# Attention and two MLP layers in one kernel on one core: another planner for the order of the instructions

## The chip, the core and the metric

The kernel runs on one core of one Trainium2 chip. A core has a matrix engine (TensorE, PE in the rows; its weight loads have a row name of their own, PEld), a vector engine (VectorE, DVE), an activation engine (ScalarE, ACT), a general engine (GpSimd, POOL), a queue that issues the transfers (SyncE, SP) and 16 DMA engines. SBUF is the on-chip memory that all of them reach; PSUM is the small memory that TensorE writes its products to, in eight banks.

The metric is the device time of one execution in microseconds (us). Three runs of the kernel before gave 600.65, 600.74 and 601.78 us; the median is 600.74 us.

## What is computed

The input is a small linear attention with a decay per head (2 batches, 8 heads, 768 positions, 64 values per head), whose output, 1536 tokens of 512 values, goes through two MLP layers with 2048 hidden values each:

```
for b in range(nb):                                  # blocks of 64 positions
    intra = einsum('bhic,bhjc->bhij', qb, kb) * Dmask
    intra = einsum('bhij,bhjd->bhid', intra, vb)
    inter = einsum('bhid,bhde->bhie', qb * lam_pow, kv_state)
    out[:, :, sl] = intra + inter
    kv_state = lam_block * kv_state + einsum('bhsd,bhse->bhde', kb * rev_pow, vb)
...
h = x @ moe_w_in                                     # layer 1
x = (h * tanh(softplus(h))) @ moe_w_out
h = maximum(x @ moe2_w_in, 0.0)                      # layer 2
x = (h * h) @ moe2_w_out
```

The weights are made by `np.random.randn(...) * ...` and reach the kernel as 64-bit floats; the kernel turns each into a 32-bit float itself.

## The kernel before

**Products in two halves.** Every operand x of a large product is kept as a rounded part (h) and the rest (l = x - h), and `mm3` (L186 to L191) makes one product out of three matrix products, h·h, h·l and l·h. Making the two parts is called a split: ACT casts x to h, and DVE or POOL subtracts (`split`, L241 to L245).

**Weights.** A slice of weights is 128x512 numbers of 64 bits (512 KB). `bits` (L220) loads it into one of five `raw` buffers and makes 32-bit floats in place, in four steps that follow each other: CA on ACT (L230, a scaled copy of the high word to `absw`), CB on DVE (L232, the low word shifted right by 29), CC on DVE (L234, the two put together), CD on DVE (L236, the sign). There are 64 slices, so each of these lines runs 64 times. A slice is then split (L243, L244).

**Attention.** `pair(i)` (L316) does two heads of one block of 384 positions: loads `kq` and `kv` (L379, L381), scores S (L340), scaling of k by powers of lambda on ACT (L344), of q on POOL (L348), updates U of the state (L334), masks on DVE (L351), the state's steps on DVE (L362, L364), outputs V (L373, L375), and the split of the result into `xh` (L400, ACT) and `xl` (L402, DVE). There are 16 pairs. The powers of lambda (`dT`, `qs`) are made on DVE by scans (L308, L309) out of `lam_t`, a 4 KB load (L297) that gives every partition the same eight numbers. Four pairs make one block of tokens `x`, which the first product of layer 1 needs.

**MLP.** Half of layer 1 (eight slices, 32 steps of `h_step`, `g_step`, `y_step`, L431 to L464) is done plainly, the first 16 steps in between the attention. The other half of layer 1 and all of layer 2 go in 24 quads (class `Quad`, L556): a 2x2 block of products of weights and tokens made with seven products p1 to p7 in place of eight, at the price of sums ahead of them (`paired` L258 for weights; `first_factors` L499 and `next_factors` L526 for tokens) and behind them (`add`, L588, DVE, which reads the product's PSUM bank). Behind the sums come the activation on ACT (L596) and the split of its result (`low`, L599; h on ACT at L606 or L609, l at L610 on DVE or POOL). The order of the seven products stands in `self.order` (L561), one for quads that are `turned` (every second of layer 1) and one for the others, layer 2 among them. Between a quad's products stand the output products (`y`) of the quad before, which are summed up by L425 on DVE. Products of layer 2 take turns in two PSUM banks, so a product waits until the sum of the one before it in that bank has read it.

**What sets the order.** No instruction is issued as the code is read. `op` (L113) records each with its engines and a duration for each, and the places that it reads and writes. `issue` (L132) then goes through all with a clock of its own: it gives each operation a due time, counted back from those that wait for it, and emits, engine by engine, the one with the earliest due time among those ready within SLACK (0.25 us). Where two engines are allowed it takes the one on which the operation starts first. Every engine then runs its instructions strictly in that order, each waiting for the semaphores of what it depends on. In this planner each engine is on its own: nothing says that an operation of DVE and one of POOL can hold each other up.

## Time and profile before

| | |
|---|---|
| median of three runs | 600.74 us |
| profiled execution | 601.85 us, span 599.9 us |
| TensorE busy | 577.1 us (96% of the span), 3448 matmul records |
| VectorE busy | 428.6 us (71%), 705 instructions |
| ScalarE busy | 319.5 us (53%), 662 instructions |
| GpSimd busy | 254.0 us (42%), 241 instructions |
| DMA | 49.88 MB, 24.4% of the 16 engines' span |

The profile is of one execution. Busy time of an engine is the union of its instructions' spans. A matmul's record begins when it starts and its end is modelled, so two that follow each other overlap in the record, and the idle time that the profile gives between two of them is somewhat less than what TensorE lost. The granted clock of TensorE (PEclk) is a share of 2.4 GHz: 1.00 is 2.4 GHz, 0.5 would be 1.2 GHz, and a number between them means that a stretch had some of both.

The kernel has four stages: attention with 16 steps of layer 1 woven in (0 to about 125 us), the other plain steps and the eight quads of layer 1 (to about 330 us), the passage to layer 2, in which layer 1's sums are finished and split again as layer 2's tokens (about 315 to 375 us), and the 16 quads of layer 2 (to the end).

### The profile page before, as it was taken

What the parts mean: (1) busy time and instruction counts of PE and PEld (TensorE: products, weight loads), DVE (VectorE), ACT (ScalarE), POOL (GpSimd) and SP (SyncE); (2) the same over time, 40 slices, a digit from 0 to 9 for tenths busy, and PEclk for the clock granted to TensorE, in tenths of its full rate; (3) what the DMA queues carried; (4) which work ended last, traced back from release to release, by engine and by line L of the source; (5) the groups of instructions that cost most, each with busy time, mean ns of one, the idle gap of its engine ahead of it and who ended that gap; (6) DMA issues with size and microseconds to landing.
All of it is one profiled execution on the core that took longest, in us unless ns stands there. A gap on an engine that the chain in (4) does not pass through costs nothing.

```text
span 599.9 us, 9221 instructions
## 1 busy us (share of the span) xinstructions
PE 577.1 (96%) x3448; PEld 528.8 (88%) x3448; DVE 428.6 (71%) x705; ACT 319.5 (53%) x662; POOL 254.0 (42%) x241
## 2 busy tenths in 40 slices
PE   6789999999999999999999988999999899999997
PEld 5668888889999999999999877889988789899886
DVE  3988477789873888569879999789458935633433
ACT  2554445466433545355465667867575655544441
POOL 2467244566680354125478595554115423100010
PEclk8899999999999999999999989999999999999999
DMA  8866553222000412023200311242120120100112
GB/s 291 311 184 212 169 161 115 72 71 72 0 1 1 176 36 71 2 73 138 72 0 1 116 60 35 72 175 61 47 105 2 70 107 1 35 1 0 54 52 107
DMA packets 15741, 49.88 MB, mean 83 GB/s; under 512 B 1872, under 2 KB 1872, under 8 KB 15696
## 3 DMA queue, kind: packets, MB, share of 16 engines
q1 hardware_dynamic: 15696, 49.29, 24.4%
q8 instruction: 27, 0.44, 0.3%
q14 instruction: 18, 0.15, 0.1%
HBM read 46.14 MB, written 3.15 MB: 82 GB/s over the span
## 4 chain that ended last, share of the span: by engine, by line
PE 72%; DVE 14%; POOL 5%; issue 4%; DMA 3%; ACT 1%; SPq 0%; POOLq 0%; DVEq 0%; ACTq 0%
PE y L189 10%; PE y L190 10%; PE y L191 9%; PE h L189 9%; PE h L191 9%; PE h L190 8%; PE X L190 2%; PE Y L189 2%; PE Y L191 2%; PE X L191 2%; PE Y L190 2%; PE X L189 2%; POOL w L244 2%; DVE u L590 2%; DVE raw L236 2%
## 5 line engine op out<-in xcount | busy, mean ns | idle before, releaser
L244 POOL TENSOR_TENSOR w<-raw,w 128x256 fp32r<-128x256 f32 (+1 forms) x72 | 82.7, 1155 | 79.8 <-ACT w L243 69.3
L590 DVE TENSOR_TENSOR u<-h,u 128x384 f32<-128x384 f32 x88 | 48.8, 554 | 55.8 <-PE h L191 55.2
L189 PE MATMUL h<-xh,w 128*128 128x384 f32 x244 | 83.7, 343 | 1.6 <-ACT w L243 1.1
L190 PE MATMUL h<-xl,w 128*128 128x384 f32 x244 | 82.9, 340 | 1.9 <-DVE xl L402 1.8
L191 PE MATMUL h<-xh,w 128*128 128x384 f32 x244 | 82.8, 339 | 1.0 <-POOL w L244 1.0
L596 ACT ACTIVATE u<-u 128x384 f32<-128x384 f32 x72 | 37.9, 527 | 72.0 <-DVE u L590 71.3
L189 PE MATMUL y<-gh,w 128*128 128x384 f32 x192 | 66.8, 348 | 0.2
L190 PE MATMUL y<-gl,w 128*128 128x384 f32 x192 | 64.6, 336 | 0.8 <-POOL gl L449 0.8
L243 ACT CAST w<-raw 128x256 fp32r<-128x256 f32 (+1 forms) x96 | 48.7, 523 | 29.3 <-DVE raw L236 20.4
L191 PE MATMUL y<-gh,w 128*128 128x384 f32 x192 | 64.3, 335 | 0.0
L234 DVE SCALAR_TENSOR_TENSOR raw<-absw,raw 128x512 uint32<-128x512 uint32 x64 | 56.9, 889 | 6.5 <-ACT absw L230 2.4
L610 POOL TENSOR_TENSOR g<-u,g 128x384 fp32r<-128x384 f32 x20 | 21.2, 1058 | 94.5 <-PE h L191 80.4
L236 DVE SCALAR_TENSOR_TENSOR raw<-raw 128x512 uint32<-128x512 uint32 x64 | 55.8, 872 | 1.0
L230 ACT ACTIVATE absw<-raw 128x512 f32<-128x512 f32 x64 | 43.0, 676 | 17.3 <-DVE raw L234 7.1
L189 PEld LDWEIGHTS h<-xh,w 128*128 128x128 f32 x244 | 46.1, 189 | 6.5 <-issue 1.2
L190 PEld LDWEIGHTS h<-xl,w 128*128 128x128 f32 x244 | 46.1, 189 | 5.0 <-DVE xl L402 2.6
L191 PEld LDWEIGHTS h<-xh,w 128*128 128x128 f32 x244 | 46.2, 189 | 1.6 <-POOL w L244 1.6
L425 DVE TENSOR_TENSOR y<-y,y 128x384 f32<-128x384 f32 (+1 forms) x72 | 39.6, 571 | 9.5 <-PE y L191 9.0
L232 DVE TENSOR_SCALAR raw<-raw 128x512 uint32<-128x512 uint32 x64 | 41.3, 646 | 2.4 <-DMA raw<-in_w2o_dram 2.2
L189 PEld LDWEIGHTS y<-gh,w 128*128 128x128 f32 x192 | 36.0, 187 | 3.1 <-DVE st L364 0.4
L190 PEld LDWEIGHTS y<-gl,w 128*128 128x128 f32 x192 | 36.1, 188 | 1.7 <-POOL gl L449 1.5
L449 POOL TENSOR_TENSOR gl<-u,gh 128x384 fp32r<-128x384 f32 x19 | 21.0, 1104 | 36.3 <-ACT gh L447 35.5
(266 smaller groups left out, 1514.3 us busy)
## 6 DMA issues: line engine op xcount, KB each, us to landing
raw<-in_w1i_dram SPq DMA_DIRECT2D x16, 512.0 KB, 4.2
raw<-in_w1o_dram SPq DMA_DIRECT2D x16, 512.0 KB, 3.9
raw<-in_w2i_dram SPq DMA_DIRECT2D x16, 512.0 KB, 4.4
raw<-in_w2o_dram SPq DMA_DIRECT2D x16, 512.0 KB, 3.8
kq<-in_qkv_dram SPq DMA_DIRECT2D x16, 384.0 KB, 4.8
kv<-in_qkv_dram SPq DMA_DIRECT2D x16, 384.0 KB, 3.3
out_dram<-y SPq DMA_DIRECT2D x12, 256.0 KB, 2.0
lam_t<-in_lam_dram SPq DMA_DIRECT2D x1, 4.0 KB, 6.8
```

The source lines that it names most:

```text
L189: pe.matmul(o, lhsT=wh, rhs=h, start=start, stop=False, **kw)
L190: pe.matmul(o, lhsT=wh, rhs=l, start=False, stop=False, **kw)
L191: pe.matmul(o, lhsT=wl, rhs=h, start=False, stop=stop, **kw)
L230: op("ACT", 0.68, lambda e: e.activation(absw[a].bitcast(F32), word.bitcast(F32)[:, :, 1], AF.Copy, scale=2.0 ** -112), R, A, after=after, ...
L232: op("DVE", 0.55, lambda e: e.tensor_scalar(lo, lo, 29, None, op0=ALU.logical_shift_right), [], R, after=last.get("bits", ()), name=f"CB{F ...
L234: op("DVE", 0.85, lambda e: e.scalar_tensor_tensor(lo, absw[a], 3, lo, ALU.logical_shift_left, ALU.bitwise_or), A, R, name=f"CC{F}.{io}")
L236: o = op("DVE", 0.85, lambda e: e.scalar_tensor_tensor(lo, hi, 0x80000000, lo, ALU.bitwise_and, ALU.bitwise_or), [], R, name=f"CD{F}.{io}")
L243: op("ACT", dur, lambda e: e.copy(v(h), v(t)), r, H_, name="H" + kw["name"])
L244: op(eng, 0, lambda e: e.tensor_tensor(v(l), v(t), v(h.bitcast(F32)), ALU.subtract), [*r, *H_], L_, due=kw.get("due", 1e9), name="L" + kw[ ...
L425: op("DVE", dur, lambda en: en.tensor_tensor(o, o, y, ALU.add), B, O, due=due, name=f"YD{layer}.{t}.{e}")
L590: op("DVE", 0.58, lambda e: e.tensor_tensor(o, a, b, ALU.add), [s for s in A + B if s not in O], O, name=f"add{self.n}")
L596: op("ACT", 0.52, lambda e: e.activation(o, i, fn), [s for s in I if s not in O], O, name=f"{name}.{self.n}")
```

## The change

Numbers of lines of the new kernel differ; the names are the same. Where rows of the new kernel are shown: L262 is the load of a weight slice (L227 before), L265 CA, L272 CB on ACT, L274 CB on DVE, L277 CC, L279 CD, L287 the subtraction of a split (L244), L315 the sums of `paired` (L272), L340 the load of lambda (L297), L351 and L352 the scans, L394 the masks, L405 and L407 the state's steps, L422 and L424 the loads of `kq` and `kv`, L443 and L445 the split into `xh` and `xl`, L468 the sums of outputs (L425), L575 those of `next_factors` (L532), L634 `add` (L590), L655 the l part behind an activation (L610).

1. The planner. Durations of single operations are set anew, most of them lower (TOP, SUB256, SUB384, SUB512, CC and CD). An operation that reads no PSUM bank is `shared`; a shared one on DVE or POOL may not begin before the shared one before it, on either of the two, has ended (less HEAD). TensorE is given 0.3 us after what it waits for (LATE), its results come 0.16 us later (TAIL), and the next instruction on an engine may begin somewhat before the end of the last (NEXT). An operation with two engines is kept off one of them where the other would end it sooner. All this is run for 27 sets of EARLY, SLACK and FAVOUR, and the order with the earliest end by the planner's clock is emitted.
2. CB may run on ACT too, as a scaled copy of the upper half of the low word (`top`), at 0.62 us there and 0.42 us on DVE.
3. The load of lambda comes ahead of the first `kq`.
4. The order of a quad's products in layer 1, with p7 and p5 next to each other; their sums now go by `both` and `sum`. Layer 2's order stays.
5. A split's buffer in a quad is taken from a list of free ones (`gfree`) and not in turn.

```diff
-LAT, LAND, SLACK = 0.2, 2.0, 0.25
+LAT, LATE, LAND, TAIL = 0.1, 0.3, 2.0, 0.16
+HEAD = {"DVE": 0.14, "POOL": 0.06}
+NEXT = {"PE": 0.0, "ACT": 0.1, "DVE": 0.08, "POOL": 0.04, "SP": 0.0, "-": 0.0}
...
-EARLY = 0.5
+EARLY, SLACK, FAVOUR = (0.0, 0.5, 1.0), (0.1, 0.25, 0.4), (0.0, 0.5, 1.0)
...
+        o.shared = not any(z[0] in bank for z in r) if shared is None else shared
...
+        def when(o, e, r):
+
+            r = max(r, free[e])
+            if o.shared and e in HEAD:
+                r = max(r, port - HEAD[e])
+            return r
...
+                for k in c[:]:
+                    for x, d in k[1].eng.items():
+                        if x != e and when(k[1], x, k[0]) + d + favour.get((x, e), 0) <= k[0] + k[1].eng[e]:
+                            c.remove(k)
+                            break
...
+            on[o], end[o] = e, r + o.eng[e] + (TAIL if e == "PE" else 0)
+            free[e] = r + o.eng[e] - NEXT[e]
+            if o.shared and e in HEAD:
+                port = free[e]
...
+        for early in EARLY:
+            for slack in SLACK:
+                for favour in FAVOUR:
+                    t, out = order(early, slack, {("DVE", "POOL"): favour, ("ACT", "DVE"): -0.3, ("DVE", "ACT"): 0.3})
...
+                    if best is None or t < best[0]:
+                        best = t, out
...
-    SUB384 = {"POOL": 1.1, "DVE": 0.6}
...
+    TOP = {"ACT": 0.62, "DVE": 0.42}
+    SUB384 = {"POOL": 1.01, "DVE": 0.55}
...
-        op("DVE", 0.55, lambda e: e.tensor_scalar(lo, lo, 29, None, op0=ALU.logical_shift_right),
-           [], R, after=last.get("bits", ()), name=f"CB{F}.{io}")
...
+        half = word.bitcast(U16)[:, :, 1]
+
+        def top(e):
+            if e is act:
+                e.activation(lo, half, AF.Copy, scale=2.0 ** -13, bias=2.0 ** -14 - 0.5)
+            else:
+                e.tensor_scalar(lo, lo, 29, None, op0=ALU.logical_shift_right)
+
+        op(TOP, 0, top, [], R, after=last.get("bits", ()), name=f"CB{F}.{io}")
...
-        o = op("SP", 1.05, lambda e: e.dma_start(out=kq[n4], in_=qkv_in[t, p, :, 0:2]), [], KQ, after=last.get("kq", ()), name=f"kq{i}")
+        o = op("SP", 1.05, lambda e: e.dma_start(out=kq[n4], in_=qkv_in[t, p, :, 0:2]), [], KQ, after=last.get("kq", last["lam"]), name=f"kq{i}")
...
-            self.order = ("p1", "p6", "p7", "p5", "p3", "p2", "p4") if turned else ("p1", "p6", "p2", "p7", "p4", "p5", "p3")
+            self.order = "p1 p6 p2 p7 p4 p5 p3" if layer else "p1 p6 p5 p7 p2 p3 p4" if turned else "p1 p6 p7 p5 p2 p4 p3"
...
-            (h, l), (H_, L_) = gsets[next_of("g", 4)]
+            k = gfree.pop(0)
+            (h, l), (H_, L_) = gsets[k]
...
+        def both(self):
+            if self.C and self.D:
+                r = self.t["r"]
+                self.add(r, self.D, r)
+                self.leave("c22", r, r)
```

**SP at the start.** The rows are the loads that SP issues first; before:

```order
L379 DMA kq_110<-in_qkv_dram 128x768
L381 DMA kv_114<-in_qkv_dram 128x768
L379 DMA kq_111<-in_qkv_dram 128x768
L297 DMA lam_t<-in_lam_dram 128x8
L381 DMA kv_115<-in_qkv_dram 128x768
```

and now:

```order
L340 DMA lam_t<-in_lam_dram 128x8
L422 DMA kq_110<-in_qkv_dram 128x768
L424 DMA kv_114<-in_qkv_dram 128x768
L422 DMA kq_111<-in_qkv_dram 128x768
L424 DMA kv_115<-in_qkv_dram 128x768
```

Lambda's load moved ahead of three loads; the others keep their order.

**DVE in the attention's first pairs**, from the first weight slice on (`raw_91`; `pm`, `mid` and `st` are masks and states of the pairs, `xl` the split result); before:

```order
L232 TENSOR_SCALAR raw_91<-raw_91 128x512
L351 TENSOR_TENSOR pm_123<-Y,dT 128x384
L364 SCALAR_TENSOR_TENSOR st_127<-mid_125,qs,y_136 64x64 x2
L362 COPY mid_125<-X 64x64
L308 SCALAR_TENSOR_TENSOR dT<-lam_t,g_108 128x128 x2
L309 SCALAR_TENSOR_TENSOR qs<-lam_t,g_108 128x128
L234 SCALAR_TENSOR_TENSOR raw_91<-absw_96,raw_91 128x512
L351 TENSOR_TENSOR pm_123<-X,dT 128x384
L364 SCALAR_TENSOR_TENSOR mid_125<-mid_125,qs,X 64x64 x2
L236 SCALAR_TENSOR_TENSOR raw_91<-raw_91 128x512
L402 TENSOR_TENSOR xl_83<-y_138,xh_79 128x384
L232 TENSOR_SCALAR raw_92<-raw_92 128x512
```

and now:

```order
L445 TENSOR_TENSOR xl_83<-y_136,xh_79 128x384
L394 TENSOR_TENSOR pm_123<-Y,dT 128x384
L407 SCALAR_TENSOR_TENSOR st_127<-mid_125,qs,y_136 64x64 x2
L394 TENSOR_TENSOR pm_123<-X,dT 128x384
L405 COPY mid_125<-X 64x64
L407 SCALAR_TENSOR_TENSOR mid_125<-mid_125,qs,X 64x64 x2
L277 SCALAR_TENSOR_TENSOR raw_91<-absw_96,raw_91 128x512
L279 SCALAR_TENSOR_TENSOR raw_91<-raw_91 128x512
L445 TENSOR_TENSOR xl_83<-y_138,xh_79 128x384
```

The shifts of the slices (L232) are gone from DVE here, and the last scans stand before these rows; ACT now has the shift of `raw0_91` between a scaling and a cast of the pairs:

```order
L387 ACTIVATE kv2_116<-kv2_116,dT_118 128x3x64 x2
L272 ACTIVATE raw0_91<-raw0_91 128x512
L443 CAST xh0_79<-y3_138 128x384
L405 COPY mid0_125<-X_133 64x64
L265 ACTIVATE absw1_97<-raw1_92 128x512
```

Of the 64 shifts ACT has 55 now (L272) and DVE 9 (L274); of the 24 that stood ahead of the first quad's first sum on DVE, three are left there. Of the 96 subtractions behind an activation in the quads, DVE had 44 and has 56, POOL had 52 and has 40. POOL's instructions go from 240 rows to 231, DVE's from 668 to 624. TensorE's instructions are the same in number and kind.

**DVE in the passage to layer 2**, between sums (`u`) that TensorE waits for; before:

```order
L590 TENSOR_TENSOR u2_100<-h0_131,u2_100 128x384
L532 TENSOR_TENSOR y1_88<-y1_88 128x384
L532 TENSOR_TENSOR y1_88<-y1_88,y0_87 128x384
L244 TENSOR_TENSOR w1_0_71<-raw3_94,w1_0_71 128x512
L244 TENSOR_TENSOR xl0_83<-y0_87,xh0_79 128x384
L590 TENSOR_TENSOR u4_102<-h0_131,u2_100 128x384
L610 TENSOR_TENSOR g1_1669<-u3_101,g0_1632 128x384
L244 TENSOR_TENSOR xl0_83<-y0_87,xh0_79 128x384
L244 TENSOR_TENSOR kq2_1087<-y1_88,kq2_1087 128x384
L532 TENSOR_TENSOR y0_87<-y0_87,y1_88 128x384
L590 TENSOR_TENSOR u5_103<-h0_131,u2_100 128x384
```

and now:

```order
L634 TENSOR_TENSOR u2_100<-h0_131,u2_100 128x384
L575 TENSOR_TENSOR y1_88<-y1_88 128x384
L575 TENSOR_TENSOR y1_88<-y1_88,y0_87 128x384
L287 TENSOR_TENSOR xl0_83<-y0_87,xh0_79 128x384
L634 TENSOR_TENSOR u4_102<-h0_131,u2_100 128x384
L287 TENSOR_TENSOR kq0_962<-y1_88,kq0_962 128x384
L287 TENSOR_TENSOR xl0_83<-y0_87,xh0_79 128x384
L634 TENSOR_TENSOR u5_103<-h0_131,u2_100 128x384
```

Between the three sums stood four and four other operations, and now three and two: a weight's subtraction (`w1_0_71`) and one behind an activation (`g1`) went to POOL, and a sum (L575) behind the last of the three.

**DVE in layer 2**, in one quad in which `paired` makes a slice's sums, between two sums (`u`) of products; before:

```order
L590 TENSOR_TENSOR u2_100<-h1_132,u2_100 128x384
L232 TENSOR_SCALAR raw2_93<-raw2_93 128x512
L234 SCALAR_TENSOR_TENSOR raw2_93<-absw1_97,raw2_93 128x512
L236 SCALAR_TENSOR_TENSOR raw2_93<-raw2_93 128x512
L272 TENSOR_TENSOR absw0_96<-raw2_93 128x256
L272 TENSOR_TENSOR absw0_96<-absw0_96,raw1_92 128x256
L590 TENSOR_TENSOR u0_98<-h1_132,u0_98 128x384
```

and now:

```order
L634 TENSOR_TENSOR u2_100<-h1_132,u2_100 128x384
L315 TENSOR_TENSOR absw0_96<-raw2_93 128x256
L315 TENSOR_TENSOR absw0_96<-absw0_96,raw1_92 128x256
L287 TENSOR_TENSOR w0_4_67<-raw1_92,w0_4_67 128x256
L634 TENSOR_TENSOR u0_98<-h1_132,u0_98 128x384
```

The slice's shift went to ACT, its CC and CD stand one sum earlier, and a subtraction stands in their place.

## Rows read from the trace of the kernel before

**Rows 1.** The page, busy time of each engine and its share of the span.
```profile
PE 577.1 (96%) x3448; PEld 528.8 (88%) x3448; DVE 428.6 (71%) x705; ACT 319.5 (53%) x662; POOL 254.0 (42%) x241
```
**Rows 2.** Busy time by stretch: start:end, length, engines in the order named first.
```profile
core 0: us, PE busy (x) PEld busy (x) DVE busy (x) ACT busy (x) POOL busy (x), PEclk, DMA share, GB/s
0.00:15.00 15.00, 9.81 (x65) 7.63 (x67) 5.11 (x15) 3.82 (x9) 3.81 (x15) 0.84 0.80 291
15.00:30.00 15.00, 11.11 (x125) 9.35 (x123) 14.45 (x35) 7.52 (x19) 6.75 (x6) 0.84 0.87 311
30.00:45.00 15.00, 12.24 (x107) 9.99 (x104) 13.36 (x24) 8.53 (x17) 9.92 (x8) 0.98 0.65 184
120.00:135.00 15.00, 14.27 (x95) 13.46 (x96) 12.66 (x14) 9.26 (x21) 10.18 (x10) 1.00 0.22 71
330.00:345.00 15.00, 14.20 (x78) 13.15 (x77) 13.79 (x25) 10.34 (x22) 7.62 (x7) 1.00 0.35 118
345.00:360.00 15.00, 13.12 (x56) 11.21 (x55) 14.93 (x16) 9.60 (x21) 14.27 (x12) 0.89 0.17 59
360.00:375.00 15.00, 13.46 (x66) 11.52 (x65) 14.67 (x22) 10.66 (x24) 8.83 (x10) 1.00 0.11 35
60.00:330.00 270.00, 268.86 (x1760) 258.07 (x1756) 207.11 (x338) 134.81 (x286) 132.80 (x122) 1.00 0.21 68
```
**Rows 3.** What weight loads waited for: us in total, times, longest.
```profile
PEld h L189 <- DVE u L590: 8.4, 8, 2.3
PEld h L190 <- DVE xl L402: 2.6, 2, 2.1
```
**Rows 4.** SP's first issues in order of time: start, us, instruction.
```profile
0.74 0.37 SPq L379 DMA_DIRECT2D kq<-in_qkv_dram  x1
...
2.10 0.43 SPq L297 DMA_DIRECT2D lam_t<-in_lam_dram  x1
```
**Rows 5.** The page's DMA issues: count, KB each, us from issue to landing.
```profile
kv<-in_qkv_dram SPq DMA_DIRECT2D x16, 384.0 KB, 3.3
out_dram<-y SPq DMA_DIRECT2D x12, 256.0 KB, 2.0
lam_t<-in_lam_dram SPq DMA_DIRECT2D x1, 4.0 KB, 6.8
```
**Rows 6.** DVE in order of time, 8 to 36 us; in brackets, idle before and releaser.
```profile
8.88 0.34 DVE L301 COPY lam_t<-lam_t 64x4 f32<-64x4 f32 x2 [7.75 <-DMA lam_t<-in_lam_dram]
...
18.28 0.42 DVE L232 TENSOR_SCALAR raw<-raw 128x512 uint32<-128x512 uint32 x1
...
32.61 1.48 DVE L234 SCALAR_TENSOR_TENSOR raw<-absw,raw 128x512 uint32<-128x512 uint32 x1
```
**Rows 7.** TensorE in order of time, 4 to 36 us.
```profile
4.89 2.77 PE L340 MATMUL y<-kq 64*128 64x128 f32 x24
...
25.36 0.45 PE L189 MATMUL h<-xh,w 128*128 128x384 f32 x1 [1.05 <-ACT w L243]
...
34.61 0.44 PE L190 MATMUL h<-xl,w 128*128 128x384 f32 x1 [1.83 <-DVE xl L402]
```
**Rows 8.** DVE in order of time, 350 to 354 us.
```profile
350.63 1.50 DVE L244 TENSOR_TENSOR w<-raw,w 128x512 fp32r<-128x512 f32 x1
352.06 1.35 DVE L244 TENSOR_TENSOR xl<-y,xh 128x384 fp32r<-128x384 f32 x1
```
**Rows 9.** TensorE in order of time, 351 to 358 us.
```profile
353.93 0.45 PE L189 MATMUL h<-dT,w 128*128 128x384 f32 x1 [1.88 <-DVE u L590]
...
355.21 0.63 PE L189 MATMUL y<-w,gh 128*128 128x512 f32 x1
```
**Rows 10.** TensorE in order of time at 466 us.
```profile
466.72 0.45 PE L189 MATMUL h<-pm,w 128*128 128x384 f32 x1 [1.50 <-DVE u L590]
```
**Rows 11.** Groups by line: out<-in, shapes, count, busy us, mean ns, idle before.
```profile
L232 DVE TENSOR_SCALAR raw<-raw 128x512 uint32<-128x512 uint32 x64 | 41.3, 646 | 2.4 <-DMA raw<-in_w2o_dram 2.2
L230 ACT ACTIVATE absw<-raw 128x512 f32<-128x512 f32 x64 | 43.0, 676 | 17.3 <-DVE raw L234 7.1 <-DMA raw<-in_w2o_dram 5.6 <-issue 2.0
```

128 lines of the change are left out of this document (69 added, 59 removed).

## The prediction

> **What bounds the kernel now.** I read the engines' busy time first, then the same by stretch, then who waited for whom, then the order of time at the longest waits. TensorE is busy 577.1 us of a span of 599.9 us [rows 1], so at most 22.8 us of idle time can be won, and whatever its granted clock costs. By stretch [rows 2] that idle time is not spread: 5.2 us in 0 to 15, 3.9 in 15 to 30, 2.8 in 30 to 45, 1.1 in all of 60 to 330, then 0.8, 1.9 and 1.5 in the three stretches from 330 to 375. Two waits stand outside that table's worst rows: 0.7 us in 120 to 135 [rows 2] and 1.5 us before 466.72 [rows 10]. The clock was 0.84 in the first two stretches and 0.89 in 345 to 360 [rows 2], that is, a part of each ran at 1.2 GHz.
>
> Where TensorE idles, VectorE is full: 14.45 and 13.36 us of 15 in 15 to 45, then 13.79, 14.93 and 14.67 in 330 to 375 [rows 2]. The weight loads waited 8.4 us for VectorE's sums of products (L590), in eight waits, and 2.6 us for the low part of x (L402) [rows 3]. So the kernel is TensorE's, and what it loses, it loses to VectorE's queue in two places and to the start.
>
> VectorE is also slower there than it need be. The shift L232 takes 0.42 us at its shortest [rows 6] and 0.646 us on average [rows 11]; a subtraction of a split takes 1.50 us at 350.63 [rows 8], and CC 1.48 us at 32.61 [rows 6], while GpSimd is busy 14.27 us of 15 [rows 2].
>
> **The change, part by part.** The sum goes against the profiled execution, 601.85 us (span 599.9 and 1.95 around it); the median of the runs, 600.74, is 1.1 us below it, and I take that off at the end.
>
> *A. The start.* VectorE's first real work is at 8.88 us, when lambda lands, after 7.75 us of waiting [rows 6]; the load was issued at 2.10 us behind three transfers of 384 KB, and took 6.8 us [rows 4, 5]. Now it has the slot of 0.74 us [rows 4]. How long it takes with nothing ahead is not in the trace. From below the nearest row is the shortest transfer, 2.0 us from issue to landing, from above its own 6.8 us [rows 5]: it lands between 2.7 and 7.5 us, so VectorE starts 1.4 to 6.2 us sooner. I take 4.5, nearer to the short end because what was ahead of it in the queue is gone, and no more because the first scores need kq, which landed at 4.89 us at the latest [rows 7] and now goes out one slot of 0.43 us later [rows 4], and the scaling needs the first kv, 3.3 us after its issue [rows 5]. From there to 34.61 us, where TensorE waited 1.83 us for the fourth pair's low part [rows 7], VectorE is full, so what leaves its queue comes off the path: three shifts stood ahead of that subtraction and all are on ScalarE now, 3 x 0.646 = 1.9 us. What is left of the idle time of 30 to 45 is 2.76 - 1.83 = 0.9 us, and I let it go, since more shifts leave there too. A clock of 0.84 over 15 us costs 2.4 us of full speed [rows 2]; with shorter waits I count 0.7 of it as won. Together 4.5 + 1.9 + 0.9 + 0.7 = 8.0 us. Bounds: 1.4 + 1.3 + 0 + 0 = 2.7 (shifts at 0.42), and 6.2 + 1.9 + 0.9 + 2.4 = 11.4.
>
> *B. 120 to 135 us.* 0.7 us of idle time [rows 2], as layer 1's first token sums are made beside the last plain steps. With nearly all of the first 24 shifts off VectorE I count all of it; bounds 0.7 lost to 0.7 won.
>
> *C. The passage.* The order puts three and two operations between three successive sums where four and four stood. One of those that left the first gap is the subtraction of 1.50 us at 350.63 [rows 8], and TensorE's wait behind it was 1.88 us [rows 9]: 1.5 of it goes. That wait was followed by a stretch at 1.2 GHz (a 512-column product's record is 0.63 us at 355.21 [rows 9]; 0.89 of the clock over 15 us is 1.65 us [rows 2]); with a wait of 0.4 us in place of 1.9 I count it gone, 1.65. That wait is all the idle time of 345 to 360; the stretches beside it have 0.80 + 1.54 = 2.3 us [rows 2], and 0.4 is left of the wait. Five of the eight shifts in that passage leave VectorE, 3.2 us at 0.646 [rows 11], so I count six tenths of these 2.7 us, 1.65. Together 4.8 us; bounds 0 and 5.9. One wait I expect to stay: late in the passage one gap keeps five operations.
>
> *D. Layer 2.* Between the two sums around 466 us stood five operations and now stand three, two of them sums of half slices: 1.3 of 1.5 us [rows 10]; bounds 0 and 1.5.
>
> *E. What ScalarE gets.* 55 shifts. The trace has no shift there; the nearest row is CA, of the same 128x512 numbers, 0.676 us [rows 11]: 37 us, on an engine that is busy 319.5 of 599.9 [rows 1]. ScalarE's idle time hides it; what it costs is a cast or an activation that queues behind one. Five stand in the first pairs and five in the passage, at most 10 x 0.676 = 6.8 us if each delays TensorE by its whole length, nothing if none does. I take 1.0 us lost, since ScalarE has 4.7 us of 15 free even at 330 to 345 [rows 2].
>
> *F. The rest.* Twelve subtractions behind activations went from GpSimd to VectorE, for the most part in layer 1's quads and late in layer 2; in 60 to 330 VectorE is busy 207.11 of 270 us and TensorE 268.86 [rows 2], so they lie beside TensorE's work: nothing, and at a subtraction's 1.35 us [rows 8], 16 us if that cover were gone. The other order of products in layer 1 moves work within those 270 us, in which TensorE idles 1.1: 0 to 0.5 won, and as much lost; I take nothing. The list of free buffers changes no operation.
>
> A sentence on the shared port. At 350 us VectorE's and GpSimd's operations are both long and both engines full [rows 2, 8], which is what holding each other up looks like. The Trainium skill ("SBUF — State Buffer", Who interferes with whom) says that an operation of VectorE with two SBUF inputs, or in a 2-port mode as a shift is, and one of GpSimd that reads SBUF exclude each other for a whole instruction. By that rule every shift taken away frees GpSimd too, and C would come to its bound of 5.9, the sum to 14.9 and the time to 585.9; the sum below does not use it.
>
> Sum: 8.0 + 0.7 + 4.8 + 1.3 - 1.0 = 13.8 us. 601.85 - 13.8 - 1.1 = 587.0 us.
>
> **The rivals.**
>
> *1. Only the start is won (593 us).* The order is fixed ahead by a clock of its own; if ScalarE's releases come otherwise than planned, a GpSimd operation gets in ahead of VectorE's where the plan had it behind, and sums wait as before. Against it: the passage loses six operations between its sums whatever the timing. For it: GpSimd's 14.27 of 15 us in 345 to 360 [rows 2] doesn't go away by order alone. Then C and D are 0: 8.0 + 0.7 - 1.0 = 7.7, 601.85 - 7.7 - 1.1 = 593.0. The Trainium skill has the rule behind this ("SBUF — State Buffer", Who interferes with whom): "Issue order, not op shape, decides who blocks."; no run here shows it yet.
>
> *2. Slower (604 us): the shift is dear on ScalarE.* It reads two bytes out of every eight and adds a constant, which no row has. In 330 to 345 four shifts ran and ScalarE had 4.66 us free [rows 2]: from 1.17 us each ScalarE is the bound there. At 2.0 us each, the 26 that lie before 170 us and in the passage are 26 x 1.3 = 34 us more than at 0.676; if half of it lands on TensorE that is 17 us, and 587.0 + 17 = 604. Against it: the row of CA, and casts of the same size are as short.
>
> *3. It doesn't do what it says (600 us).* Lambda takes its 6.8 us wherever it stands, kq comes later by it, and VectorE stays the queue that sets the start: A is 1.4, E takes 1.0 of it back, B, C and D stay: 601.85 - 0.4 - 1.1 = 600.3.
>
> **How the numbers follow.** A measurement can tell about 0.2% from no change, 1.2 us. The forecast has 0.70, with a range of its own from 580 to 592; rival 1 has 0.15, rival 3 has 0.07, rival 2 has 0.08. Best case, all upper bounds: 11.4 + 0.7 + 5.9 + 1.5 = 19.5, 581.2 us, and 579 with the part of each wait that the modelled ends hide. The range goes from 579 to 597, over rival 1 and short of 2 and 3. Faster: 0.70 + 0.15 and a part of rival 3, 0.87; same, the rest of rival 3, 0.05; slower 0.08.
>
> **What would show it.** A: lambda's scans start near 4.4 us and the first product of layer 1 at 18 to 20 us (25.36 before [rows 7]). C: TensorE busy over 14.4 of 15 us, at a clock of 1.00, around the passage's middle, and fewer than 4 us of waits for the sums. D: no wait over 0.5 us there. E: the shift on ScalarE at 0.6 to 0.7 us; over 1.17 us and rival 2 is on. It is wrong if the scans start after 6 us, if a wait of 1.5 us for a sum is still there in mid-passage, or if new waits, for ScalarE above all, stand where none did.

## The result and the profile after

The changed kernel takes 582.74 us (median of four runs, 581.49 to 583.02), the kernel before, run beside it, 600.69 us: a ratio of 0.9697, with a 95% interval of 0.9674 to 0.9719. The forecast was 587.0 us with a range of 579 to 597. The profiled execution took 583.02 us, with a span of 581.2 us where it was 599.9 [rows 1].

By stretch, as in [rows 2] (us; busy time of PE, PEld, DVE, ACT, POOL, each with its instructions, then the granted clock, the DMA share and GB/s):

```profile
0.00:15.00 15.00, 11.54 (x118) 9.33 (x118) 10.87 (x29) 5.95 (x14) 5.99 (x18) 1.00 0.85 311
15.00:30.00 15.00, 12.90 (x122) 11.02 (x123) 13.39 (x31) 9.21 (x20) 7.70 (x7) 0.77 0.90 339
...
330.00:345.00 15.00, 14.86 (x75) 13.17 (x75) 14.26 (x19) 12.03 (x27) 14.43 (x12) 1.00 0.22 71
345.00:360.00 15.00, 15.00 (x76) 13.54 (x75) 13.91 (x20) 10.84 (x25) 10.80 (x11) 1.00 0.11 36
360.00:375.00 15.00, 14.69 (x73) 12.89 (x72) 14.23 (x21) 13.79 (x30) 10.22 (x10) 1.00 0.33 105
```

TensorE now idles 3.5 us in the first stretch and 0.5 in the three of the passage together, where it idled 5.2 and 4.2. What is left is at the start: 2.1 us in 15 to 30, which also has a stretch at 1.2 GHz (0.77). VectorE is still full in the passage: 42.4 us of 45, where it was 43.4 [rows 2] (the same stretches of time, though the changed kernel is 10 to 17 us ahead in its work there). It is not that VectorE has less to do; its work stands otherwise.

VectorE's start and the first large product:

```profile
3.74 0.34 DVE L344 COPY lam_t<-lam_t 64x4 f32<-64x4 f32 x2 [2.61 <-DMA lam_t<-in_lam_dram]
4.11 0.74 DVE L351 TENSOR_TENSOR_SCAN dT<-lam_t,g 128x128 f32<-128x128 f32 x2
...
19.09 0.44 PE L223 MATMUL h<-xh,w 128*128 128x384 f32 x1 [1.14 <-ACT w L286]
```

The weight loads' waits for sums (us in total, times, longest):

```profile
PEld h L223 <- DVE u L634: 2.3, 5, 0.7
```

The shift on each engine (nanoseconds: shortest, median, longest; then the first and last start in us):

```profile
L272 ACT ACTIVATE raw<-raw x55: 647/667/702, 13.1 to 495.3; 128x512 uint32<-128x512 uint16 x55
...
L274 DVE TENSOR_SCALAR raw<-raw x9: 413/418/1240, 39.6 to 427.2; 128x512 uint32<-128x512 uint32 x9
```

The waits for sums (L634) fell from 8.4 us [rows 3] to 2.3. The shift costs 0.667 us on ScalarE and no more at its longest than 0.702; the nine left on VectorE still go from 0.413 to 1.240.

**Where the gain lies.** A way to read two traces against each other that needs no idle times: take the start of the k-th large product (384 or 512 columns; both traces have 2736 of them) in each, and subtract. The difference was 6.3 us at the first (25.36 before [rows 7], 19.09 after), 0.4 at the sixth, 7.9 at the 25th, 9.7 in the middle of layer 1, 10.3 at 318 us of the kernel before, 16.9 at 383, 18.6 at the end. (The dip at the sixth is for the most part one of order: products of the attention, which come later before, stand from 21.1 to 26.3 us between the third and the fourth large product; TensorE was granted 1.2 GHz there, from 20.4 to 27.3 us.) So of 18.6 us, 10.3 come before the passage, 6.6 in it, 1.7 in layer 2. The table below gives the same three parts for every run.

### The profile page after: what moved, and what is told of

The parts are those of the page before. It is cut to its first block, busy times and chain, and to the rows that moved or that the text cites. A ratio compares the mean times of both kernels' runs of the same rounds, so it can differ in the third digit from the quotient of the medians.

```text
span 581.2 us, 9201 instructions
## 1 busy us (share of the span) xinstructions
PE 570.7 (98%) x3448; PEld 527.0 (91%) x3448; DVE 402.2 (69%) x659; ACT 347.2 (60%) x717; POOL 247.4 (43%) x232
## 4 chain that ended last, share of the span: by engine, by line
PE 82%; DVE 8%; ACT 5%; DMA 3%; issue 1%; POOL 0%; SPq 0%; ACTq 0%; DVEq 0%
PE y L223 12%; PE y L224 11%; PE y L225 11%; PE h L223 9%; PE h L225 9%; PE h L224 9%; PE X L224 2%; PE Y L223 2%; PE X L225 2%; PE Y L224 2%; PE X L223 2%; PE Y L225 2%; PE X L383 1%; PE Y L418 1%; DVE raw L279 1%
## 5 line engine op out<-in xcount | busy, mean ns | idle before, releaser
L287 POOL TENSOR_TENSOR w<-raw,w 128x256 fp32r<-128x256 f32 (+1 forms) x68 | 76.5, 1134 | 61.3 <-ACT w L286 50.3
L634 DVE TENSOR_TENSOR u<-h,u 128x384 f32<-128x384 f32 x88 | 48.7, 553 | 55.3 <-PE h L225 53.6
L655 POOL TENSOR_TENSOR g<-u,g 128x384 fp32r<-128x384 f32 x19 | 20.9, 1098 | 120.8 <-PE h L225 109.5
L277 DVE SCALAR_TENSOR_TENSOR raw<-absw,raw 128x512 uint32<-128x512 uint32 x64 | 53.3, 833 | 10.6 <-ACT raw L272 9.6
L286 ACT CAST w<-raw 128x256 fp32r<-128x256 f32 (+1 forms) x96 | 48.3, 521 | 20.4 <-DVE raw L279 9.9
L279 DVE SCALAR_TENSOR_TENSOR raw<-raw 128x512 uint32<-128x512 uint32 x64 | 57.2, 894 | 1.4
L265 ACT ACTIVATE absw<-raw 128x512 f32<-128x512 f32 x64 | 42.9, 672 | 17.9 <-DMA raw<-in_w2o_dram 5.7
L468 DVE TENSOR_TENSOR y<-y,y 128x384 f32<-128x384 f32 (+1 forms) x72 | 40.8, 570 | 14.5 <-PE y L225 14.4
L655 DVE TENSOR_TENSOR gl<-u,gh 128x384 fp32r<-128x384 f32 x33 | 22.0, 667 | 27.4 <-ACT u L652 23.0
L492 POOL TENSOR_TENSOR gl<-u,gh 128x384 fp32r<-128x384 f32 x23 | 26.1, 1140 | 30.8 <-ACT gh L490 30.8
L272 ACT ACTIVATE raw<-raw 128x512 uint32<-128x512 uint16 x55 | 36.8, 669 | 0.0
```

Source lines behind the costliest of these rows:

```text
L265: op("ACT", 0.68, lambda e: e.activation(absw[a].bitcast(F32), word.bitcast(F32)[:, :, 1], AF.Copy, scale=2.0 ** -112), R, A, after=after, ...
L277: op("DVE", 0.7, lambda e: e.scalar_tensor_tensor(lo, absw[a], 3, lo, ALU.logical_shift_left, ALU.bitwise_or), A, R, name=f"CC{F}.{io}")
L279: o = op("DVE", 0.7, lambda e: e.scalar_tensor_tensor(lo, hi, 0x80000000, lo, ALU.bitwise_and, ALU.bitwise_or), [], R, name=f"CD{F}.{io}")
L286: op("ACT", dur, lambda e: e.copy(v(h), v(t)), r, H_, name="H" + kw["name"])
L287: op(eng, 0, lambda e: e.tensor_tensor(v(l), v(t), v(h.bitcast(F32)), ALU.subtract), [*r, *H_], L_, due=kw.get("due", 1e9), name="L" + kw[ ...
L468: op("DVE", dur, lambda en: en.tensor_tensor(o, o, y, ALU.add), B, O, due=due, name=f"YD{layer}.{t}.{e}")
```

## The experiments

The first theory is the prediction's: lambda first and the shifts off VectorE relieve its queue, and the new order of the passage follows from that. The rival: the planner's new rule, that a `shared` operation of VectorE and one of GpSimd (neither reads a PSUM bank) can't overlap, is what brings the time, and the relief by itself little. This rule is called the port rule, or the rule, from here on. Runs whose name begins with b_ are the kernel before with parts added; those with a_ are the changed kernel with parts taken away, and with the planner's set (EARLY 1.0, SLACK 0.1, FAVOUR 1.0, the one that its search takes) written in.

| run | what it is | us | ratio (95%) | to 318 us | passage | layer 2 |
|---|---|---|---|---|---|---|
| after | the change | 582.74 | 0.967 to 0.972 | 10.3 | 6.6 | 1.7 |
| b_lam | before, lambda first | 599.56 | 0.996 to 0.999 | 0.4 | 0.1 | 0.0 |
| b_lam_shift | the same, shift also on ScalarE | 592.15 | 0.984 to 0.989 | 5.7 | 2.7 | 1.5 |
| b_rule_alone | before, port rule and short durations | 589.08 | 0.980 to 0.983 | 3.6 | 8.0 | 2.0 |
| b_port_dve | the same, lambda first | 581.18 | 0.966 to 0.970 | 10.4 | 8.0 | 2.0 |
| b_port | the same, shift also on ScalarE | 579.32 | 0.963 to 0.969 | 12.8 | 8.0 | 2.0 |
| b_rule_pad | b_port with the old, longer durations | 584.27 | 0.971 to 0.977 | 10.9 | 5.9 | 2.0 |
| a_dve_shift | after, all shifts on VectorE | 586.14 | 0.974 to 0.978 | 10.7 | 5.1 | 0.5 |
| a_lam_late | after, lambda in its old place | 591.41 | 0.983 to 0.988 | 3.8 | 6.7 | 1.7 |
| a_old_order | after, old order of products | 582.78 | 0.969 to 0.975 | 11.0 | 6.6 | 1.0 |
| a_set | after, the old planner's constants and FAVOUR 0 | 586.92 | 0.975 to 0.979 | 8.1 | 4.6 | 1.4 |
| a_old_dur | after, no rule, long durations | 604.85 | 1.004 to 1.010 | 3.8 | -3.3 | -0.9 |
| a_no_port | after, no rule, short durations | 613.54 | 1.018 to 1.024 | -6.5 | -3.5 | -1.4 |

The last three columns are us won against the trace of before, at the large products that started there at 318.67 and 383.37 us, and at the last. They come from one execution each, that of before 1.1 us over its median, so their sum differs from the difference of the medians by 0.4 to 4.4 us. The ratio is to the kernel before, run beside each.

### Lambda first, alone

```diff
-        op("SP", 0.45, load_lam, [], ["lam"], name="lam")
+        last["lam"] = [op("SP", 0.45, load_lam, [], ["lam"], name="lam")]
...
-        o = op("SP", 1.05, lambda e: e.dma_start(out=kq[n4], in_=qkv_in[t, p, :, 0:2]), [], KQ, after=last.get("kq", ()), name=f"kq{i}")
+        o = op("SP", 1.05, lambda e: e.dma_start(out=kq[n4], in_=qkv_in[t, p, :, 0:2]), [], KQ, after=last.get("kq", last["lam"]), name=f"kq{i}")
```

> The kernel before with one change: lambda's load is issued first. If the wait for lambda is what the start loses (term A's first 4.5 us), the scans start near 4 us in place of 8.88 and the whole is 3 to 6 us shorter, 595 to 598 us. If VectorE's full queue behind it is the real bound up to 50 us, the early start is used up by the next wait and the whole stays at 599 to 601 us.

599.56 us: the rival. The first product of layer 1 starts at 21.84 us, 3.5 sooner than before, and by 56 us all of that is gone. The largest single loss is one wait of TensorE: its score product goes into a PSUM bank that the subtraction of x's low part has to read first. VectorE ahead of it, then GpSimd in the same time, then TensorE (start us, length us; in brackets what ended the idle time before):

```profile
32.85 0.68 DVE L236 SCALAR_TENSOR_TENSOR raw<-raw 128x512 uint32<-128x512 uint32 x1
33.45 1.24 DVE L232 TENSOR_SCALAR raw<-raw 128x512 uint32<-128x512 uint32 x1
34.72 1.38 DVE L234 SCALAR_TENSOR_TENSOR raw<-absw,raw 128x512 uint32<-128x512 uint32 x1
36.13 1.67 DVE L236 SCALAR_TENSOR_TENSOR raw<-raw 128x512 uint32<-128x512 uint32 x1
37.72 0.55 DVE L402 TENSOR_TENSOR xl<-Y,xh 128x384 fp32r<-128x384 f32 x1
```

```profile
27.96 1.30 POOL L244 TENSOR_TENSOR w<-raw,w 128x512 fp32r<-128x512 f32 x1 [3.60 <-ACT w L243]
29.22 1.01 POOL L348 TENSOR_TENSOR qd<-kq,qs 128x384 f32<-128x384 f32 x1
33.23 1.17 POOL L449 TENSOR_TENSOR gl<-u,gh 128x384 fp32r<-128x384 f32 x1 [3.00 <-ACT gh L447]
34.37 1.18 POOL L348 TENSOR_TENSOR qd<-kq,qs 128x384 f32<-128x384 f32 x1
35.51 1.74 POOL L244 TENSOR_TENSOR w<-raw,w 128x512 fp32r<-128x512 f32 x1
37.28 1.39 POOL L449 TENSOR_TENSOR gl<-u,gh 128x384 fp32r<-128x384 f32 x1
```

```profile
38.32 0.58 PE L340 MATMUL Y<-kq 64*128 64x128 f32 x1 [2.74 <-DVE xl L402]
```

Read them side by side: three of VectorE's operations on `raw` take 1.24, 1.38 and 1.67 us. GpSimd's end at 34.40, 35.55 and 37.25; VectorE's end at 34.69, 36.10 and 37.80. That is GpSimd's end plus their own length alone (0.42 [rows 6], 0.68 in the first row here), less 0.13 us each time: each waits for GpSimd's to end and then runs. GpSimd's rows at 34.37 and 35.51 lengthen by the same turns: 35.55 is VectorE's end at 34.69 plus the 1.01 us of such an operation at 29.22, and 37.25 is 36.10 plus the 1.30 of the one at 27.96, each less 0.15 us. The operation behind them, which reads a PSUM bank, takes its 0.55 although GpSimd is busy all through it. The old planner had counted 0.55 + 0.85 + 0.85 = 2.25 us for the three; they took 4.29, and the urgent one stood behind them. TensorE was granted 1.2 GHz from 38.2 us, where the wait ends, to 45.0, and what was left of the gain went in that stretch. This trace is of the slowest of ten executions (601.22 us), so how much of the 3.5 us the wait takes in the others is not shown; what is shown is that the median is 1.0 us below the kernel before.

### The shift on ScalarE, without the new planner

```diff
-        op("DVE", 0.55, lambda e: e.tensor_scalar(lo, lo, 29, None, op0=ALU.logical_shift_right),
-           [], R, after=last.get("bits", ()), name=f"CB{F}.{io}")
+        op({"ACT": 0.62, "DVE": 0.55}, 0, top, [], R, after=last.get("bits", ()), name=f"CB{F}.{io}")
```

> The kernel before, old planner and old durations, with lambda first and the shift allowed on ScalarE too (36 of 64 go there by the old planner's rule). If what VectorE is relieved of makes the gain, this gets most of it: the start whole, some 8 us, and 2 to 4 us of the passage, 588 to 591 us. If the gain is the new planner's, it stays where lambda alone leaves it, 595 to 598 us.

592.15 us, between the two. The old planner moves 36 of the 64 shifts. Relief is worth 7.4 us over lambda alone, 5.3 of the 9.3 us in the traces before 318 us (of which up to 3.4 can be the clock's: up to 45 us, 17.1 us of b_lam's trace are at 1.2 GHz and 10.2 of this one's); but a wait of 1.7 us for a sum stays in the passage. VectorE there (L597 is `add`), then TensorE:

```profile
346.22 0.55 DVE L597 TENSOR_TENSOR u<-h,u 128x384 f32<-128x384 f32 x1
346.68 0.88 DVE L617 TENSOR_TENSOR g<-u,g 128x384 fp32r<-128x384 f32 x1
347.49 1.37 DVE L251 TENSOR_TENSOR kq<-y,kq 128x384 fp32r<-128x384 f32 x1
348.78 1.67 DVE L539 TENSOR_TENSOR y<-y,y 128x384 f32<-128x384 f32 x1
350.37 1.37 DVE L251 TENSOR_TENSOR kq<-y,kq 128x384 fp32r<-128x384 f32 x1
351.66 0.55 DVE L597 TENSOR_TENSOR u<-h,u 128x384 f32<-128x384 f32 x1
```

```profile
353.66 0.45 PE L189 MATMUL h<-xh,qs 128*128 128x384 f32 x1 [1.68 <-DVE u L597]
```

Four operations from SBUF to SBUF between two sums, 5.3 us by their records for what takes 2.2 when nothing is beside it (0.54 and 0.55 in the rows at 352.13 and 352.60 us). The sums themselves keep their 0.55; the one that TensorE waits for is the next, at 353.06 us, behind all of these.

### The shifts back on VectorE, in the changed kernel

```diff
-    TOP = {"ACT": 0.62, "DVE": 0.42}
+    TOP = {"DVE": 0.42}
```

> The new kernel with all 64 shifts on VectorE again, the planner with the set of numbers that it took in the new kernel. If the relief of VectorE counts, the start loses 2 to 3 us, 120 to 170 us loses about 1, the passage 2 to 4: 588 to 591 us. If the planner's knowledge of the shared port counts, TensorE's waits stay as short as they are and it takes 583 to 585 us.

586.14 us, between both expectations and nearer to the second: 55 shifts on ScalarE are worth 3.4 us here (2.4 in the traces, all from 318 us on). At the start they are worth nothing that shows, though that comparison is blurred: the changed kernel's trace has 6.8 us at 1.2 GHz from 20.4 us, this one has none before its last product. The weight loads' waits for sums from 320 to 400 us are 4.5 us, in the changed kernel 2.3:

```profile
PEld h L223 <- DVE u L634: 4.5, 5, 1.4
```

### The port rule off, in the changed kernel

```diff
             r = max(r, free[e])
-            if o.shared and e in HEAD:
-                r = max(r, port - HEAD[e])
             return r
```

> The new kernel with a planner that doesn't hold an operation of VectorE or GpSimd back for one of the other; all else, the set of numbers too, as in the new kernel. If the shared port's model makes the gain behind the start, the waits for the sums return in 315 to 375 us and in layer 2, 6 to 9 us, 589 to 592 us. If lighter queues make it, the order is about as good, 583 to 585 us.

613.54 us: neither. I had not thought that the other parts of the change could be a loss by themselves. Without the rule the planner believes in 0.55 us for a sum or a subtraction on VectorE wherever it stands, so it gives VectorE more of them (GpSimd is busy 202.9 us in place of 247.4), and queues them ahead of sums (L632 is `add`, L573 a sum of `next_factors`):

```profile
352.74 0.91 DVE L573 TENSOR_TENSOR y<-y,y 128x384 f32<-128x384 f32 x1
353.68 1.27 DVE L573 TENSOR_TENSOR y<-y 128x384 f32<-128x384 f32 x1
354.99 1.25 DVE L573 TENSOR_TENSOR y<-y,y 128x384 f32<-128x384 f32 x1
356.17 1.64 DVE L573 TENSOR_TENSOR y<-y 128x384 f32<-128x384 f32 x1
357.84 1.23 DVE L573 TENSOR_TENSOR y<-y,y 128x384 f32<-128x384 f32 x1
358.99 0.55 DVE L632 TENSOR_TENSOR u<-h,u 128x384 f32<-128x384 f32 x1
```

```profile
359.59 0.45 PE L221 MATMUL h<-pm,w 128*128 128x384 f32 x1 [3.37 <-DVE u L632]
```

Five in a row take 6.3 us where 2.75 were planned, and TensorE waits 3.4 us behind them. The weight loads' waits for sums come to 11.2 us in this run. The passage is 10.1 of the 29.9 us between this trace and the changed kernel's, though; 16.8 are lost before it. Five waits of TensorE from 124 to 162 us, four for low parts on VectorE and GpSimd and one for a cast, come to 5.6 us, and three for sums of outputs (L466) from 290 to 328 us to 4.0; the rest of the 16.8 I have not placed.

### The rule off, but with the old, longer durations

```diff
...
-    SUB384 = {"POOL": 1.01, "DVE": 0.55}
+    SUB384 = {"POOL": 1.1, "DVE": 0.6}
...
-        op("DVE", 0.7, lambda e: e.scalar_tensor_tensor(lo, absw[a], 3, lo, ALU.logical_shift_left, ALU.bitwise_or),
+        op("DVE", 0.85, lambda e: e.scalar_tensor_tensor(lo, absw[a], 3, lo, ALU.logical_shift_left, ALU.bitwise_or),
...
-    SUM = {"DVE": 0.55, "POOL": 1.01}
+    SUM = {"DVE": 0.8, "POOL": 1.1}
```

> The changed kernel without the port rule, but with the longer durations of the kernel before, which had some of the holding-up averaged into them. Beside the run without the port rule and with the short durations (613.5 us), it tells whether that run lost its 31 us for want of the rule or because nothing at all stood for the contention. If longer durations are as good a forecast as the rule: 583 to 586. If the rule is what matters: 590 to 600. If both are nothing and something else broke there: over 608.

604.85 us, outside all three expectations: 8.7 better than with short durations and still slower than the kernel before (by 0.4 to 1.0%), whose durations it has. Longer durations stand in for a part of the rule, not for the rule: 22 us remain. Why this is slower even than before, I have not separated; it has the later starts for TensorE, the preference between engines and the constants of the search, none of which was made for a plan without the rule.

### The rule in the old planner

The other way round: before, with lambda and the shift as above, plus the rule and the short durations, and nothing else of the change.

```diff
-                f = free[e]
-                r0 = max(f, min(r for r, _ in c))
-                pick = min((x for x in c if x[0] <= r0 + SLACK), key=lambda x: (x[1].due, max(x[0], f)))
-                r = max(f, pick[0])
+                c = [(max(r, free[e], port - HEAD[e] if o.shared and e in HEAD else 0.0), o) for r, o in c]
+                r0 = min(r for r, _ in c)
+                pick = min((x for x in c if x[0] <= r0 + SLACK), key=lambda x: (x[1].due, x[0]))
+                r = pick[0]
...
             free[e] = o.end
+            if o.shared and e in HEAD:
+                port = o.end
```

> The kernel before with lambda first, the shift allowed on ScalarE, the new short durations and the rule of the shared port in its old planner; nothing else of the change (no later start for TensorE, no search over 27 sets, no other order of products). Two theories for the 9.4 us between the changed kernel (582.7) and the run with lambda and the shift alone (592.2): by the first it is the port rule that makes the difference, and this comes to 583 to 586 us with the waits for layer 2's sums nearly gone; by the second it is the rest of the new planner and the new order of products, and this stays at 590 to 593.

579.32 us, beyond the first theory's number and the best of all. The passage by stretch:

```profile
330.00:345.00 15.00, 15.00 (x76) 13.50 (x75) 12.10 (x16) 13.10 (x27) 13.82 (x12) 1.00 0.11 37
345.00:360.00 15.00, 15.00 (x76) 13.41 (x75) 10.76 (x16) 10.56 (x22) 9.24 (x9) 1.00 0.11 36
360.00:375.00 15.00, 15.00 (x76) 13.54 (x75) 10.75 (x21) 12.35 (x26) 5.33 (x6) 1.00 0.19 70
```

TensorE doesn't idle at all from 45 to 480 us. VectorE waits in the passage now, where TensorE waited for it, ahead of the first of these sums for a product and ahead of the second, by its row, for GpSimd:

```profile
347.24 0.56 DVE L602 TENSOR_TENSOR u<-h,u 128x384 f32<-128x384 f32 x1 [1.09 <-PE h L196]
347.71 1.00 DVE L544 TENSOR_TENSOR y<-y,y 128x384 f32<-128x384 f32 x1
348.64 0.55 DVE L256 TENSOR_TENSOR kv<-y,kv 128x384 fp32r<-128x384 f32 x1
350.74 0.56 DVE L602 TENSOR_TENSOR u<-h,u 128x384 f32<-128x384 f32 x1 [1.56 <-POOL kv L256]
```

Two operations between two sums, and VectorE free 1.1 and 1.6 us ahead of them. The holding-up itself is still there: the mean of CC and CD, each with the same 64 instructions, first in b_lam_shift, then here:

```profile
L241 DVE SCALAR_TENSOR_TENSOR raw<-absw,raw 128x512 uint32<-128x512 uint32 x64 | 58.1, 908 | 8.0 <-ACT raw L236 5.6 <-issue 0.5
L243 DVE SCALAR_TENSOR_TENSOR raw<-raw 128x512 uint32<-128x512 uint32 x64 | 55.8, 872 | 1.3
```

```profile
L248 DVE SCALAR_TENSOR_TENSOR raw<-raw 128x512 uint32<-128x512 uint32 x64 | 55.2, 862 | 1.3
L246 DVE SCALAR_TENSOR_TENSOR raw<-absw,raw 128x512 uint32<-128x512 uint32 x64 | 52.4, 818 | 4.4 <-ACT raw L241 2.9
```

908 to 818 and 872 to 862 ns: 6.4 us less in 128 instructions, a quarter of the 26.9 us that they took beyond 0.68 each. So the rule keeps the two engines apart only in part. What it does besides, as I read it, is to let the plan know how long they will be, so that no sum is put behind a queue that looks short; a_set below, with less holding-up and a longer time, speaks for that.

### The rule alone, the rule without the shift, the rule without the short durations

```diff
-        op({"ACT": 0.62, "DVE": 0.42}, 0, top, [], R, after=last.get("bits", ()), name=f"CB{F}.{io}")
+        op("DVE", 0.42, lambda e: e.tensor_scalar(lo, lo, 29, None, op0=ALU.logical_shift_right),
+           [], R, after=last.get("bits", ()), name=f"CB{F}.{io}")
```

for b_port_dve, and for b_rule_alone also `after=last.get("kq", ())`, lambda's old place; b_rule_pad is b_port with the durations of the kernel before.

> The kernel before with the short durations and the rule of the shared port in its own planner, and nothing else: lambda stays where it was, every shift stays on VectorE. With lambda and the shift on ScalarE the same planner came to 579.3 us, 12.8 below the same kernel without rule and durations. If the rule pays by itself: 586 to 590. If it pays only once VectorE's queue is shorter and starts sooner, as with lambda (1.1 us in the kernel before, 8.7 in the changed one): 595 to 601.

> The run with the rule in the old planner (579.3 us), with all shifts back on VectorE. What the shifts on ScalarE are worth: without the rule they brought 7.4 us (599.6 to 592.2), in the changed kernel 3.4 (586.1 to 582.7). If the rule does part of the same work, 582 to 584, lost at the start and in the passage; if their worth adds to the rule's, 586 to 588.

> The run with the rule in the old planner (579.3 us), with the kernel before's longer durations in place of the short ones: the rule alone. If the rule is what matters, 579 to 583; if it was the durations, 588 to 592 (592.2 without either).

The rule with its durations, alone, brings 11.6 us (589.08), as its first expectation had it. It wins the whole 8.0 of the passage and 2.0 of layer 2, both the same with or without lambda and the shift; more can't be won there by waiting less, since TensorE doesn't idle from 318 to 480 us in any of the three traces. Only the time to 318 us differs between these three runs: 3.6, then 10.4 with lambda first, then 12.8 with the shift. So with the rule lambda is worth 7.9 us (589.08 to 581.18) and the shift 1.9 (581.18 to 579.32), which the intervals (0.966 to 0.970 and 0.963 to 0.969) don't tell from nothing; without it they were worth 1.0 and 7.4. The expectation that the shift would bring 3 to 5 under the rule was too high. The rule with the old durations comes to 584.27, between its two expectations and nearer to the first: 7.9 of the 12.8 us between b_lam_shift and b_port are the rule's, and this is the pair of runs that differ by the rule and nothing else; 5.0 need the short durations as well. Short durations without the rule were tried in the new planner only.

### Lambda late, in the changed kernel

```diff
-        o = op("SP", 1.05, lambda e: e.dma_start(out=kq[n4], in_=qkv_in[t, p, :, 0:2]), [], KQ, after=last.get("kq", last["lam"]), name=f"kq{i}")
+        o = op("SP", 1.05, lambda e: e.dma_start(out=kq[n4], in_=qkv_in[t, p, :, 0:2]), [], KQ, after=last.get("kq", ()), name=f"kq{i}")
```

> The changed kernel with lambda's load in its old place behind three transfers of 384 KB. My prediction counted 4.5 us for lambda alone, and alone in the kernel before it gave 1.1. If VectorE's queue swallowed it there and the shorter queue now lets it through, this loses 3 to 4.5 us: 586 to 587.5, first product of layer 1 at 22 to 23.5 us. If lambda is worth nothing in either kernel: 582.5 to 584.

591.41 us, 8.7 lost, more than either expectation and than the 4.9 us by which lambda is there sooner (DVE's copy of it starts at 3.74 us in the changed kernel, at 8.66 here, at 8.88 before [rows 6]). TensorE, with two waits of over 3 us that the changed kernel doesn't have:

```profile
10.61 0.58 PE L383 MATMUL X<-kq 64*128 64x128 f32 x1 [3.58 <-DMA kq<-in_qkv_dram]
...
26.62 0.69 PE L418 MATMUL y<-pm,kv 128*64 128x128 f32 x4 [3.37 <-DVE pm L394]
...
30.75 0.69 PE L223 MATMUL h<-xh,w 128*128 128x384 f32 x1
```

The first is for the third `kq`. SP issues it at 3.05 us in both kernels, but it lands later where lambda's small load stands in the queue shortly ahead of it. From issue to landing, in us, in the changed kernel and then here:

```profile
kq<-in_qkv_dram SPq DMA_DIRECT2D x1, 384.0 KB, 6.2
```

```profile
kq<-in_qkv_dram SPq DMA_DIRECT2D x1, 384.0 KB, 7.5
```

The kernel before had this wait too:

```profile
10.82 0.58 PE L340 MATMUL X<-kq 64*128 64x128 f32 x1 [3.16 <-DMA kq<-in_qkv_dram]
```

The second is for a mask that VectorE starts at 26.01 us, behind three steps of weight slices (1.8 us from 23.24 us on):

```profile
23.24 0.68 DVE L277 SCALAR_TENSOR_TENSOR raw<-absw,raw 128x512 uint32<-128x512 uint32 x1
...
26.01 0.56 DVE L394 TENSOR_TENSOR pm<-y,dT 128x384 f32<-128x384 f32 x1
```

The ring of four `kq` buffers is full as well, since the first is not freed until its pair has used it, which waits for lambda's powers: SP issues nothing from 7.9 to 11.2 us. That by itself costs little: the two loads behind it go out 3.8 and 3.3 us later than in the changed kernel and land 1.3 and 0.1 us later. TensorE was granted 1.2 GHz from 8.9 us on, within the first wait, to 19.2, and again from 26.0 us, within the second, to 32.8. The first product of layer 1 is at 30.75 us instead of 19.09; of these 11.7 us, 6.5 are left at the end of the attention.

### The order of products, and the set of constants

```diff
-            self.order = "p1 p6 p2 p7 p4 p5 p3" if layer else "p1 p6 p5 p7 p2 p3 p4" if turned else "p1 p6 p7 p5 p2 p4 p3"
+            self.order = "p1 p6 p7 p5 p3 p2 p4" if turned else "p1 p6 p2 p7 p4 p5 p3"
```

```diff
-EARLY, SLACK, FAVOUR = (0.0, 0.5, 1.0), (0.1, 0.25, 0.4), (0.0, 0.5, 1.0)
+EARLY, SLACK, FAVOUR = (0.5,), (0.25,), (0.0,)
```

> The changed kernel with layer 1's quads in their old order of products. I put the order at nothing (within 0.5 us): 582.3 to 583.5. The rival: the passage's 6.6 us, of which I had foreseen 4.8, rests in part on p7 and p5 being next to each other, so that sums of layer 1 are done sooner; then 584.5 to 587, lost between 315 and 375 us.

> The changed kernel with the old planner's constants (EARLY 0.5, SLACK 0.25) and no favour for VectorE in place of the set that its search takes (1.0, 0.1, 1.0). The changed kernel is 3.4 us slower than its port rule in the old planner. If that is because the set with the earliest end by the planner's clock is not the best on the chip: 578 to 581. If it is the finer clock itself (later starts for TensorE, tails, overlaps): 582 to 585.

The order of products is worth nothing: 582.78 us, the passage 6.6 as in the changed kernel. The old constants in the new planner come to 586.92 us, outside both expectations: they cost 4.2 us, so the search does choose better than those; that is not why the changed kernel is behind b_port. This run also moves work: GpSimd is busy 115.1 us, 247.4 in the changed kernel, and VectorE runs 785 instructions, not 659 (I put that down to FAVOUR 0, which was not set by itself). CC and CD are shorter in it than in any other run, 764 and 775 ns on average against 833 and 894 in the changed kernel, and still the passage wins 2.0 us less: less holding-up doesn't by itself make the better plan. In the traces the changed kernel and b_port are 4.2 us apart (3.4 by their medians): 2.5 are lost before 318 us (the stretch at 1.2 GHz from 20.4 us is in there), 1.4 in the passage and 0.3 in layer 2. What in the finer clock does it, later starts for TensorE, tails or preferences between engines, was not tried.

## Why the prediction came out as it did

The time fell 4.3 us below the forecast and well inside the range. Step by step:

**A, the start: 8.0, and B, 0.7.** Together 8.7, measured 9.7 in the middle of layer 1. The scans start at 4.11 us (4.4 foretold), the first product at 19.09 (18 to 20). The size held; the split did not, so that the sum came this near is in part luck. Lambda was to bring 4.5 and the shifts 1.9. Lambda alone brings 1.0, and under the rule 7.9 to 8.7; the shifts bring 7.4 without the rule, 1.9 with it in the old planner, and in the changed kernel 3.4, none of it before 318 us. The step that failed was adding up what each takes off VectorE's queue, as if each microsecond were free of the others: lambda's 3.5 us are there in b_lam and are lost again, the largest part at one wait, whose cause was in the rows of before, the long operations of [rows 6]. Three sizes in A were off besides. The three shifts were priced at the mean of all 64, 0.646 us; in that place they take 0.42 each (18.28 [rows 6], 25.12 and 29.79 us), which is A's own lower bound of 1.3. The 0.7 for the clock is 1.7 in these two traces: half of the difference between 10.2 us at 1.2 GHz up to 31 us before and 6.8 after. And A looked at lambda's wait on VectorE alone: TensorE's longest wait of the start was the 3.16 us for the third `kq`, and it went because that load, too, lands sooner with lambda's first.

**C, the passage: 4.8, measured 6.6.** The wait of 1.88 us and the stretch at 1.2 GHz [rows 9] went, as counted, and TensorE is busy 15.00 us in 345 to 360 at a clock of 1.00. The mis-sized term is the last, 1.65 of 2.7 us for the stretches beside it and what was left of the wait: 2.3 went and 0.45 is left. That makes 5.4 with the other terms; the remaining 1.2 us show as no idle time in these rows, and I have not traced them. That five shifts leave was the reason given for the last term, and it is not the main one: with all shifts on VectorE and lambda late, the rule with its durations brings 8.0 us in the passage, relief alone 2.7.

**D, layer 2: 1.3, measured 1.7.** No wait for a sum stands near 450 us now, where this place is. The rule with its durations, alone, brings 2.0.

**E, the price on ScalarE: 1.0 lost.** At 0.667 us a shift (0.6 to 0.7 foretold, 0.676 assumed) ScalarE's idle time covers them: behind the first shift (13.1 us) TensorE has one wait for ScalarE of over 0.25 us, 1.14 before 19.09, and the kernel before had the same one, 1.05 [rows 7]. The shifts are a gain or nothing in each comparison. The term should have been nothing.

**F: nothing for the order of products and for the moved subtractions.** The first is shown by a_old_order. The second wasn't tried by itself.

**The sentence on the shared port**, which the sum did not use, was the better half. The Trainium skill ("SBUF — State Buffer", Who interferes with whom) says that an operation of VectorE with two SBUF inputs and one of GpSimd that reads SBUF exclude each other, and that VectorE with one SBUF input outside its 2-port modes doesn't contend. The trace agrees with both halves:

```profile
L634 DVE TENSOR_TENSOR u<-h,u x88: 543/557/558, 195.5 to 568.6; 128x384 f32<-128x384 f32 x88
...
L277 DVE SCALAR_TENSOR_TENSOR raw<-absw,raw x64: 676/693/1846, 16.9 to 496.0; 128x512 uint32<-128x512 uint32 x64
```

88 sums that read one operand from PSUM never took over 558 ns, though 26 of them had operations of GpSimd beside them for all or nearly all of their length; CC, from SBUF alone, took up to 1846.

**The rivals.** Rival 1, that sums wait as before because the order comes from the planner's own clock, was wrong for this planner and right in kind for one without the rule: in a_no_port one row of five operations is 3.6 us longer than planned, and TensorE waits 3.4 us behind it. Whether a release of ScalarE's that comes otherwise than planned is behind that, as the rival had it, was not looked at. Rival 2 fell with 0.702 us as the longest shift. Rival 3 fell with lambda's landing in 3.0 us against 6.8 [rows 5].
